# Last groups of the layer-1 backward attention: where wq, K and w2 are loaded and turned

## The chip, the cores and the metric

One core of a Trainium2 chip runs one program. The metric is the device time of a run in microseconds (us), smaller is better. The kernel before took 1139.64 us, median of three runs (1136.17 to 1146.07). One execution was taken by the hardware profiler; all times inside it are us from the start of its span.

Engine names: PE is the matrix engine (PEld its weight loads), DVE the vector engine, ACT the scalar engine, POOL the general-purpose one, SP the engine that issues the loads; SPq is a load issue on SP.

## What is computed

Two layers are run forward and back. The backward pass of attention needs, for each group (batch b, key head kv), the caches V and K and a quarter of wq:

```python
def _A_ref(x, k_cache, v_cache, wq, wo):
    q = (x @ wq).reshape(B, Sq, Hq, Dh).transpose(0, 2, 1, 3)   # B=2, Sq=1, Hq=32, Dh=128
    k = jnp.repeat(k_cache, rep, axis=1)                        # 4 key heads, Sk=16384
    v = jnp.repeat(v_cache, rep, axis=1)
    p = softmax(einsum("bhqd,bhkd->bhqk", q, k) * Dh ** -0.5)
    o = einsum("bhqk,bhkd->bhqd", p, v)
    return o.transpose(0, 2, 1, 3).reshape(B, Sq, Hq * Dh) @ wo
def _B_ref(x, w1, b1, w2, b2):
    return gelu(layernorm(x) @ w1 + b1) @ w2 + b2
...
for layer in (0, 1):
    x = x + _A_ref(layernorm(x), ...)
    x = x + _B_ref(layernorm(x), ...)
```

The outputs are x after both layers and the gradients of a given grad_out by x, the caches and the weights. All data is bfloat16.

## The kernel before, in words

The order of work: forward of both layers, then backward of the MLP of layer 1, of its attention (`attn_bwd`, called once, with l = 1), of the MLP of layer 0 (`w2b`, then `weights_down`), and last a long stage that makes all the gradients of the caches and weights while it runs the attention of layer 0 back.

**Tiles and buffers.** Every load brings one tile of 128 x 4096 bfloat16 (1 MB) into the pool `ld`, which has `NLD` = 7 buffers. All loads are issued by SP, one after the other in the order in which the program allocates the tiles. A new tile takes the free buffer that was released first, and SP waits until the last reader of that buffer's former tile is done. So the place of a load in the program fixes its place in SP's order and the buffer it gets; the time at which it starts is set by the release of that buffer.

**`attn_bwd`** goes over seven groups in the order 0, 4, 3, 1, 5, 2, 6 (group 7 has its tiles kept on the chip and is woven into groups 3 and 1). A group has four chunks of V and four of K. In this document V6.1 is chunk 1 of V of group 6, K6.3 is chunk 3 of its K, and so on. wq comes in quarters, one for each pair of groups with the same kv, and each quarter in two halves: wq1.0 and wq1.4 are the first and second half of quarter 1, wqL.0 and wqL.4 those of the last quarter (kv = 2), w2.0 to w2.6 the tiles of w2 that the next stage needs.

The work is written out by slots, numbered 0 to 127, and then some more until all queues are empty. Slot s transposes a quarter of a V chunk on PE (`emit_T`, L480, eight transposes) and copies it out on ACT or DVE (L159, L162); it runs what the schedule `Sched` has for the slot (`run_slot`); and it makes the scores of slot s - 2 (L726). `later(n, f)` puts f into slot s + n; the queue `q` gives one item every other slot, and one every slot while more than four are waiting or after the last slot. Groups 2 and 6 lie in slots 96 to 127.

- `post` (after a chunk's last scores) makes dX, and `queue_acc` queues two *quads* for the chunk (L512: eight matmuls of dX with K each), and after the last chunk the evacuation of the sum, `reduce` (L527) and `finish`. K of a chunk is loaded when its first quad is run (L469). For the last group, 6, it is loaded already in `post` (`accs[g].pre`), and after the last chunk the first five tiles of w2 are loaded there too (`ahead.load`).
- `finish` puts dq of the group aside. When both groups of a kv are done, `wq_now` deals with its quarter of wq: both halves are loaded in the slot after it (L961), the eight rows of the quarter are turned on DVE (L269, 32 x 32 blocks) in slots +7 to +14, and the two products on PE (L296) are in slots +12 and +17.
- The last quarter is treated apart (`wq_steps`, L986): its halves are loaded from slot 113 on, and its eight rows are turned by transposes on PE (L358, tile `wtq`) and copied out by ACT or DVE. `wq_q` holds these steps; one of them is run in every second slot, so they spread over slots 113 to 125. After group 6 its `finish` copies dq (L1004) and makes the last products (L995, `dn_ps`).
- `ahead` is the object `w2b`. A *unit* of a w2 tile is a forward product on PE (L337) and a turn on DVE (L269) or PE. After the last slots `ahead.some(0, 1)` runs the four units of w2.0, one in each of four slots.

When `attn_bwd` has ended, w2.5 and w2.6 are loaded, the remaining units of w2.0 are run, `banks` clears two accumulators on DVE (L394, L397), and `attn_in_bwd` starts the layer norm backward (L232 on) from dn; the products of w2 follow.

Of the kernel before, what the change touches and what calls it, by code (L numbers as in the profile page):

```python
# [23 lines left out]
def kernel(  # L24
# [36 lines left out]
    DJ = D // 128  # L61
# [5 lines left out]
    NCH = T // TC  # L67
# [3 lines left out]
    CP = TC // 2  # L71
# [3 lines left out]
    NLD = 7  # L75
# [18 lines left out]
    def pt(shape, dtype, name):  # L94
        return ps_tp.tile(shape, dtype, name=name, tag="tp")

    def px(shape, dtype, name):
        return ps_x.tile(shape, dtype, name=name, tag="x")
# [4 lines left out]
    def pm_(shape, dtype, name):  # L103
        return ps_sm.tile(shape, dtype, name=name, tag="sm")
# [35 lines left out]
    def charge(eng, us):  # L140
        load[eng] += us
# [322 lines left out]
    def kv_load(w, g, c):  # L464
        keep = w + str(c) if g == G - 1 else w if (g, c) == (XG, 0) else None
        t = held_tiles[keep] if keep else ld.tile([128, LDW], BF16, name="kv_" + w, tag="ld")
        if keep not in held:
            src = Kv if w == "K" else Vv
            nc.sync.dma_start(t[:].rearrange("p (t d) -> p t d", d=128), src[g, :, c * TC:(c + 1) * TC, :])  # L469
            if keep:  # L470
                held.add(keep)
        return t[:].rearrange("p (t d) -> p t d", d=128)
# [78 lines left out]
    def queue_acc(sc_, a, c_list, tail, coef=None):  # L551
        for c in c_list:
            for q in range(NB // 2):
                sc_.q.append(lambda c=c, q=q: a.quad(c, q, coef))
        if tail:
            def fin():
                a.evac()
                sc_.later(2, a.reduce)
            sc_.q.append(fin)
# [93 lines left out]
    def attn_bwd(l, do_bf, dqT, dn, groups, ahead):  # L653
        sch = Sched()
        wq_q, wq_n = deque(), {}
        slots = []
        for i, g in enumerate(groups):
            for c in range(NCH):
                for b in range(NB):
                    slots.append((g, c, b))  # L660
                    if 2 <= i < 2 + NCH // 2 and c % 2 == 0:
                        slots.append((G - 1, (i - 2) * 2 + c // 2, b))
        kTs, sc, accs = {}, {}, {}
        made = {"n": 0}
        done_g = []
        both = pm_([128, 512], F32, "acc2")
        Acc.third = both[:, 0:256]
        V.memset(both[:, 256:512], 0.0)

        def wq_job(kv):  # L670
            return wq_turned(l, kv, dqT, both[:, 256:512], lambda: px([128, 512], F32, "spg"))

        def wq_now(kv):
            n = wq_job(kv)
            n[1]()
            for f in n[0]:
                sch.later(1, f)
            for j in range(DJ):
                sch.later(7 + j, n[2][j])
            for k in range(2):  # L680
                sch.later(12 + 5 * k, n[3][k])
            if kv == groups[-3] % HKV:
                sch.later(19, wq_sum)

        def wq_sum():
            fin = px([128, DJ, 2], F32, "dn_fin")
            columns(both[:, 256:512], fin)
            V.tensor_copy(out=dn[:], in_=fin[:])

        def post(g, c):  # L690
            dp = sc.pop((g, c))
            PE.matmul(dp[:].rearrange("p h t -> p (h t)"), lhsT=hot3[:],
                      rhs=dlr[:, g, l, :].unsqueeze(2).to_broadcast([128, 8, TC]), start=False, stop=True)
            k = made["n"]
            made["n"] += 1
            ds = dXr[k // 2 % 3][:, :, k % 2]
            ev = e_all[:, g, c * CP:(c + 1) * CP, l, :, :].rearrange("p a h b -> p h a b")
            V.tensor_tensor(out=ds.rearrange("p a h b -> p h a b"),
                            in0=dp[:].rearrange("p h (a b) -> p h a b", b=2), in1=ev, op=ALU.mult)
            charge("D", 0.5)  # L700
            if c == 0:
                def finish(ps, g=g):
                    V.tensor_scalar(out=dqT[:, g, :], in0=ps, scalar1=QSCALE, scalar2=None, op0=ALU.mult)
                    done_g.append(g % HKV)
                    if g == groups[-1]:
                        wq_n["last"][1]()
                        wq_n["last"][3]()
                    elif done_g.count(g % HKV) == 2:
                        wq_now(g % HKV)
                accs[g] = Acc(g, "K", None, finish, 2 if g == G - 1 else groups.index(g) % 2)  # L710
            acc = accs[g]
            if g == groups[-1]:
                accs[g].pre[c] = kv_load("K", g, c)
                if c == NCH - 1:
                    for k in range(NLD - 2):
                        ahead.load(k)
            coef = lambda u: ds[:, u - c * CP].rearrange("p h t -> p (h t)")
            sch.later(2, lambda: queue_acc(sch, acc, [c], c == NCH - 1, coef))

        def score(s):  # L720
            g, c, b = slots[s]
            if b == 0:
                sc[g, c] = px([128, 8, TC], F32, "dp")
            kT = kTs.pop(s)
            for j in range(8):
                PE.matmul(sc[g, c][:, :, b * 8 + j], lhsT=kT[:, j, :], rhs=do_bf[:, g, :], start=(b + j == 0),  # L726
                          stop=False)
            if b == NB - 1:
                post(g, c)

        cv = None
        s = 0
        v_turns = deque(lambda c=c, b=b: turn(held_tiles["V%d" % c][:, b * 1024:(b + 1) * 1024],
                                              lambda: pt([128, 8, 128], BF16, "turn"))
                        for c in range(NCH) for b in range(NB))
        while s < len(slots) + 2 or sch.busy():
            sch.s = s
            if s < len(slots):
                g, c, b = slots[s]
                if g == G - 1:  # L740
                    kTs[s] = kept_vT(c)[:, b * 8:(b + 1) * 8, :]
                else:
                    if b == 0:
                        cv = kv_load("V", g, c)
                    kTs[s] = emit_T(cv, b, True)
                    if s % 3 == 2 and s >= 8 and v_turns:
                        v_turns.popleft()()
                if g == groups[-1] and b == 1 and c == 0:
                    n = wq_n["last"] = wq_steps(l, g % HKV, dqT, dn, lambda: pt([128, 8, 128], BF16, "wtq"),
                                                lambda: px([128, 512], F32, "dn_ps"))  # L750
                    for k, f in enumerate(n[0]):
                        wq_q.append(lambda f=f, k=k, n=n: (f(), n[2][4 * k]()))
                        wq_q.extend(n[2][4 * k + 1:4 * k + 4])
            sch.run_slot(1 if s < len(slots) else 2)
            if 2 <= s < len(slots) + 2:
                score(s - 2)
            if wq_q and (s % 2 == 1 or len(wq_q) > 6):
                wq_q.popleft()()
            if s > len(slots) + 2:
                ahead.some(0, 1)  # L760
            s += 1
        assert not wq_q

# [188 lines left out]
    def wq_turned(l, kv, dqT, acc, bank):  # L952

        hs = slice(kv * 8, kv * 8 + 8)
        box = {}
        Gq = g_tile(8, True)

        def load(j):
            wt = ld.tile([128, LDW], BF16, name="wqt", tag="ld")
            box[j] = wt[:].rearrange("p (j n) -> p j n", j=4)  # L960
            nc.sync.dma_start(box[j], wq_v[:, j:j + 4, kv * D:(kv + 1) * D])  # L961

        def turn_row(j):
            turn32(box[j - j % 4][:, j % 4, :])

        def dq_in():
            for b in range(2):
                V.tensor_copy(out=dq_all[:, hs, 2 * l + b], in_=dqT[:, b * HKV + kv, :])
            spread_g(dq_all[:, hs, 2 * l:2 * l + 2], 0, 8, Gq, bank())

        def part(j):
            products(box[j], Gq, 0, acc[:, 32 * j:32 * j + 128])

        return ([lambda j=j: load(j) for j in (0, 4)], dq_in, [lambda j=j: turn_row(j) for j in range(DJ)],
                [lambda j=j: part(j) for j in (0, 4)])
# [406 lines left out]
    sch = Sched()  # L1382
    kTs, dps, accs, ready = {}, {}, {}, []
# [127 lines left out]
    while 2 * m < NS + 2:  # L1511
# [7 lines left out]
        for k in range(2):  # L1519
            s = 2 * m + k  # L1520
            if s < NS:
                i, b = NCH + s // NB, s % NB
# [38 lines left out]
    i, g = NC - 1, order[-1]  # L1561
# [58 lines left out]
```

## Time and profile before

| what | value |
|---|---|
| runs | 1139.64, 1136.17, 1146.07 us |
| span of the profiled execution, first to last instruction | 1138.1 us |
| mean granted PE clock | 0.857 |
| PE, DVE, ACT busy | 915.9 (80%), 619.8 (54%), 534.0 (47%) us |
| moved by DMA | 449.20 MB, mean 395 GB/s |
| the chain that ended last, by engine | PE 45%, DMA 35%, DVE 10%, issue 5%, ACT 4% |
| median time from issue to landing of a K tile, over the program | 13.0 us |

How to read it: the profiled execution has only its span as its own time; the median of the runs is 1.5 us above it. Busy shares are means over stages with different limits, so a stage is read by its own window. `attn_bwd` lies from about 490 to 662 us, `w2b` and `weights_down` up to about 733 us, the last stage from there to the end.

### The profile page before, as it was taken

The page shows a single profiled execution, that of the slowest core. Times are in us where ns is not written, and L with a number is a line of the kernel's source. Part 1 is how long each engine was busy: PE and PEld are TensorE (multiplying, and loading weights), DVE is VectorE, ACT ScalarE, POOL GpSimd, SP SyncE. Part 2 cuts the span into 40 slices and gives each one's busy share as a digit, 9 for nine tenths or more (in the row PEclk, how much of TensorE's full clock was granted, in tenths as well). Part 3 has the DMA queues.
Part 4 walks back from the last instruction along what each step waited for, and adds up shares of the span by engine and source line. Part 5 has one row for each costly group of instructions (what it writes and reads, how often), then busy time and mean ns, then how long its engine had stood idle before and what let it go on. Part 6 is the DMA issues. An engine that isn't in the chain of part 4 may idle for free.

```text
span 1138.1 us, 38123 instructions
## 1 busy us (share of the span) xinstructions
PE 915.9 (80%) x16766; PEld 674.7 (59%) x16767; DVE 619.8 (54%) x1363; ACT 534.0 (47%) x1356; POOL 70.2 (6%) x124
## 2 busy tenths in 40 slices
PE   4979795468888975789887678888898897899996
PEld 3867674358766754778765567755545454455552
DVE  1545451180545523654442246678798767786876
ACT  0544351005544420434333214468697766676764
POOL 0000000000000000000000000022121111111210
PEclk9988895567999875899998678999999978897978
DMA  8999999999999979999999699998999999999997
GB/s 371 423 425 425 424 424 413 395 413 423 423 425 423 412 288 404 388 422 421 399 413 393 232 380 309 370 386 302 403 419 421 421 419 424 423 411 421 423 385 290
DMA packets 104183, 449.20 MB, mean 395 GB/s; under 512 B 7238, under 2 KB 11334, under 8 KB 66896
## 3 DMA queue, kind: packets, MB, share of 16 engines
q1 hardware_dynamic: 86672, 354.46, 77.6%
q0 software_dynamic: 17344, 92.29, 19.6%
q8 instruction: 131, 2.15, 0.7%
q14 instruction: 36, 0.29, 0.1%
HBM read 348.14 MB, written 98.58 MB: 393 GB/s over the span
## 4 chain that ended last, share of the span: by engine, by line
PE 45%; DMA 35%; DVE 10%; issue 5%; ACT 4%; POOL 0%; SPq 0%; DVEq 0%; ACTq 0%; POOLq 0%
DMA kv_V<-in_A_v_cache_dram 13%; PE tp L480 10%; DMA wt<-in_B_w_dram 5%; PE acc_all L512 4%; PE tpm L1527 4%; DMA kv_K<-in_A_k_cache_dram 4%; PE xm L1336 4%; DMA wt<-in_A_wo_dram 3%; DMA out_dram<-keepK 3%; DMA keepK<-in_A_v_cache_dram 3%; PE sc L633 3%; PE xm L1250 2%; PE wtp L358 2%; PE dp L1389 2%; PE dp L726 2%
## 5 line engine op out<-in xcount | busy, mean ns | idle before, releaser
L159 ACT COPY kT<-tp 128x512 int32<-128x512 int32 x200 | 117.4, 587 | 298.4 <-PE tp L480 289.1
L162 DVE COPY kT<-tp 128x1024 bf16<-128x1024 bf16 x168 | 114.9, 690 | 141.8 <-PE tp L480 130.4
L480 PE MATMUL tp<-ident,kv_K 128*128 128x128 bf16 x1728 | 142.0, 230 | 6.9 <-DMA kv_K<-in_A_k_cache_dram 6.8
L480 PEld LDWEIGHTS <-kv_K 128*128 128x128 bf16 x1728 | 107.8, 103 | 7.7 <-DMA kv_K<-in_A_k_cache_dram 7.5
L170 DVE CAST big<-xm 128x512 bf16<-128x512 f32 x133 | 86.3, 684 | 19.3 <-PE xm L1336 14.3
L167 ACT CAST big<-xm 128x512 bf16<-128x512 f32 x151 | 82.1, 595 | 25.0 <-PE xm L1336 14.8
L633 PE MATMUL sc<-qT_bf,kT 128*128 128x8 bf16 x2048 | 91.5, 171 | 0.1
L633 PEld LDWEIGHTS <-kT 128*128 128x128 bf16 x2048 | 75.7, 97 | 26.7 <-issue 20.8
L337 PEld LDWEIGHTS <-wt 128*128 128x128 bf16 x1920 | 57.4, 104 | 54.7 <-issue 17.8
L167 ACT CAST keepV<-xm 128x512 bf16<-128x512 f32 (+1 forms) x137 | 75.0, 594 | 29.5 <-PE xm L1336 18.5
L480 PE MATMUL tp<-ident,kv_V 128*128 128x128 bf16 x864 | 70.2, 227 | 14.1 <-DMA kv_V<-in_A_v_cache_dram 12.2
L597 ACT ACTIVATE e_all<-sc,negm 128x64 bf16<-128x64 f32 x256 | 77.2, 343 | 1.0 <-DVE negm L592 1.0
L170 DVE CAST keepV<-xm 128x512 bf16<-128x512 f32 (+1 forms) x101 | 65.9, 684 | 18.9 <-PE xm L1336 12.7
L269 DVE STREAM_TRANSPOSE wt<-wt 128x512 int32<-128x512 int32 x104 | 63.6, 674 | 14.2 <-PE w2b_f L337 11.0
L512 PE MATMUL acc_all<-kv_V,e_all 128*16 128x256 bf16 x864 | 46.0, 293 | 28.7 <-DMA kv_V<-in_A_v_cache_dram 14.4
L159 ACT COPY wt<-wtp 128x512 int32<-128x512 int32 x72 | 40.3, 587 | 57.0 <-PE wtp L358 54.1
L480 PEld LDWEIGHTS <-kv_V 128*128 128x128 bf16 x864 | 55.2, 101 | 16.2 <-DMA kv_V<-in_A_v_cache_dram 13.1
L597 ACT ACTIVATION_READ_ACCUMULATOR e_all<-sc,negm 128x1 f32 x256 | 59.8, 234 | 0.0
L167 ACT CAST keepK<-xm 128x512 bf16<-128x512 f32 x98 | 53.0, 596 | 14.1 <-PE xm L1336 7.5
L1389 PE MATMUL dp<-wdo,kT 128*128 128x64 bf16 x896 | 52.8, 206 | 0.0
L358 PE MATMUL wtp<-ident,wt 128*128 128x128 bf16 x576 | 47.8, 244 | 4.9 <-ACT wt L159 2.6
L1336 PE MATMUL xm<-QmK,blk 64*128 64x512 bf16 x256 | 48.8, 444 | 2.3 <-ACT keepV L167 1.0
(387 smaller groups left out, 1564.4 us busy)
## 6 DMA issues: line engine op xcount, KB each, us to landing
kv_K<-in_A_k_cache_dram SPq DMA_DIRECT2D x81, 1024.0 KB, 13.0
kv_V<-in_A_v_cache_dram SPq DMA_DIRECT2D x81, 1024.0 KB, 12.9
wt<-in_B_w_dram SPq DMA_DIRECT2D x42, 1024.0 KB, 12.9
wt<-in_A_wo_dram SPq DMA_DIRECT2D x32, 1024.0 KB, 9.6
out_dram<-big POOLq DMA_DIRECT2D x26, 1024.0 KB, 18.9
out_dram<-keepV POOLq DMA_DIRECT2D x19, 1024.0 KB, 20.7
out_dram<-keepK POOLq DMA_DIRECT2D x17, 1024.0 KB, 17.8
wt<-in_A_wq_dram SPq DMA_DIRECT2D x16, 1024.0 KB, 11.0
```

Of the source, the lines that this page charges most:

```text
L159: S.copy(out=dst.bitcast(I32), in_=src.bitcast(I32))
L162: V.tensor_copy(out=dst, in_=src)
L167: S.copy(out=dst, in_=src)
L170: V.tensor_copy(out=dst, in_=src)
L269: V.transpose(out=w, in_=w)
L358: PE.transpose(tp[:, o, :], view[:, o * 128:(o + 1) * 128], ident[:])
L480: PE.transpose(tp[:, j, :], cv[:, b * 8 + j, :], ident[:])
L512: PE.matmul(self.acc[cg:cg + 16, :], lhsT=coef(u), rhs=self.cv[:, t:t + 2, :].rearrange("p t d -> p (t d)"), start=False, stop=True, tile_ ...
L597: S.activation(out=e_all[:, g, f * half:(f + 1) * half, l, h, :], in_=sc[g][f][:, h, :].rearrange("p (a b) -> p a b", b=2), func=ACT.Exp, ...
L633: PE.matmul(sc[g][f][:, :, t % TH], lhsT=kT[:, j, :], rhs=q_bf[:, g, :], start=True, stop=True)
L1336: PE.matmul(pss[k][:], lhsT=blk[p:p + 64, o + 2 * h + k // 2, :], rhs=Qm[p:p + 64, :, :].rearrange("p a b -> p (a b)"), start=True, stop=T ...
L1389: PE.matmul(dp[:, :, t:t + 4], lhsT=kT[:, j, :], rhs=wd[:, :, x:x + 4], start=(b + j == 0), stop=False)
```

## The change

All of it is in `attn_bwd`.

- The quarters 0, 3 and 1 of wq are loaded and turned half by half: half k is loaded in slot +1 + 4k, its four rows are turned in slots +4 + 4k to +7 + 4k, its product is in slot +9 + 4k. The sum of the products (`wq_sum`) comes in slot +15 in place of +19.
- K of group 6 is no longer loaded in `post`; like K of the other groups it is loaded when its first quad is run. Its quads are queued one slot earlier.
- The last quarter's steps begin in slot 120 in place of 113, and one is run in every slot.
- The five w2 tiles are loaded after the quads of K6.3, from the same queue. The four units of w2.0 are no longer run in the last slots; one of them is run in `finish`, between the copy of dq and the last products, the other three after `attn_bwd`.

```diff
         def wq_now(kv):
             n = wq_job(kv)
             n[1]()
-            for f in n[0]:
-                sch.later(1, f)
-            for j in range(DJ):
-                sch.later(7 + j, n[2][j])
             for k in range(2):
-                sch.later(12 + 5 * k, n[3][k])
+                sch.later(1 + 4 * k, n[0][k])
+                for j in range(4):
+                    sch.later(4 + 4 * k + j, n[2][4 * k + j])
+                sch.later(9 + 4 * k, n[3][k])
             if kv == groups[-3] % HKV:
-                sch.later(19, wq_sum)
+                sch.later(15, wq_sum)
...
                     if g == groups[-1]:
                         wq_n["last"][1]()
+                        ahead.some(0, 1)
                         wq_n["last"][3]()
...
             acc = accs[g]
-            if g == groups[-1]:
-                accs[g].pre[c] = kv_load("K", g, c)
+            coef = lambda u: ds[:, u - c * CP].rearrange("p h t -> p (h t)")
+            def queue():
+                queue_acc(sch, acc, [c], False, coef)
+                if g == groups[-1] and c == NCH - 1:
+                    sch.q.append(lambda: [ahead.load(k) for k in range(NLD - 2)])
                 if c == NCH - 1:
-                    for k in range(NLD - 2):
-                        ahead.load(k)
-            coef = lambda u: ds[:, u - c * CP].rearrange("p h t -> p (h t)")
-            sch.later(2, lambda: queue_acc(sch, acc, [c], c == NCH - 1, coef))
+                    queue_acc(sch, acc, [], True)
+
+            sch.later(1 if g == groups[-1] else 2, queue)
...
-                if g == groups[-1] and b == 1 and c == 0:
+                if g == groups[-1] and b == 0 and c == 2:
                     n = wq_n["last"] = wq_steps(l, g % HKV, dqT, dn, lambda: pt([128, 8, 128], BF16, "wtq"),
                                                 lambda: px([128, 512], F32, "dn_ps"))
...
-            if wq_q and (s % 2 == 1 or len(wq_q) > 6):
+            if wq_q:
                 wq_q.popleft()()
-            if s > len(slots) + 2:
-                ahead.some(0, 1)
             s += 1
```

The order in which SP issues its loads, from V6.0's neighbourhood on (up to K2.0 the two orders differ in one place: wq3.4 stands ahead of V5.2 before, and behind it after):

```
before: ... K2.0 wq1.0 wq1.4 V6.0 K2.1 wqL.0 K2.2 V6.1 K6.0 K2.3 wqL.4 V6.2 K6.1 V6.3 K6.2 K6.3 w2.0 w2.1 ...
after:  ... K2.0 wq1.0 V6.0 K2.1 wq1.4 K2.2 V6.1 K2.3 V6.2 wqL.0 V6.3 K6.0 wqL.4 K6.1 K6.2 K6.3 w2.0 w2.1 ...
```

## The prediction

> **What bounds the kernel now.** I read the granted clock and the DMA rows of the page first, then the windows of the stages around the change (columns: us, busy time of PE, PEld, DVE, ACT, POOL with counts, granted PE clock, DMA share, GB/s):
>
> ```profile
> 490.00:612.00 122.00, 105.66 (x2436) 87.28 (x2432) 53.44 (x124) 46.05 (x81) 0.00 (x0) 1.00 1.01 414
> 612.00:622.00 10.00, 7.46 (x89) 5.90 (x89) 1.60 (x3) 1.76 (x3) 0.00 (x0) 0.51 0.97 384
> 622.00:660.00 38.00, 24.04 (x427) 19.22 (x424) 10.24 (x21) 9.06 (x16) 0.00 (x0) 0.72 0.72 260
> 660.00:690.00 30.00, 25.31 (x654) 22.21 (x655) 14.30 (x36) 7.41 (x13) 0.00 (x0) 0.73 1.02 369
> 690.00:733.00 43.00, 34.55 (x867) 30.88 (x867) 29.75 (x94) 18.52 (x35) 0.71 (x1) 0.92 0.91 331
> ```
>
> Up to 612 the attention is bound by its loads: DMA share 1.01, and a tile of 1.05 MB at 414 to 425 GB/s takes 2.5 us. From 622 to 660 the rate is 260 GB/s, and PE is not the bound either (24.04 of 38 us, at clock 0.72). Both wait for each other. The timeline of SP's issues says why (start, duration, issue, count; a duration over 0.4 spans waits between merged issues):
>
> ```profile
> 603.28 0.38 SPq L986 DMA_DIRECT2D wqt<-in_A_wq_dram  x1
> 607.43 0.33 SPq L469 DMA_DIRECT2D kv_K<-in_A_k_cache_dram  x1
> 608.17 0.33 SPq L469 DMA_DIRECT2D kv_V<-in_A_v_cache_dram  x1
> 620.26 2.23 SPq L469 DMA_DIRECT2D kv_K<-in_A_k_cache_dram  x2
> 624.03 0.38 SPq L986 DMA_DIRECT2D wqt<-in_A_wq_dram  x1
> 631.60 0.33 SPq L469 DMA_DIRECT2D kv_V<-in_A_v_cache_dram  x1
> 638.29 0.33 SPq L469 DMA_DIRECT2D kv_K<-in_A_k_cache_dram  x1
> 638.72 0.37 SPq L469 DMA_DIRECT2D kv_V<-in_A_v_cache_dram  x1
> 642.81 8.90 SPq L469 DMA_DIRECT2D kv_K<-in_A_k_cache_dram  x2
> ```
>
> In SP's order these are wqL.0, K2.2, V6.1, then K6.0 and K2.3, wqL.4, V6.2, K6.1, V6.3, K6.2 and K6.3. After V6.1 SP issues nothing for 12.1 us. The chain of waits goes through these loads:
>
> ```profile
> 603.28 14.46 DMA wqt<-in_A_wq_dram
> 622.16 7.58 DMA kv_K<-in_A_k_cache_dram
> 631.60 4.61 DMA kv_V<-in_A_v_cache_dram
> 638.72 8.10 DMA kv_V<-in_A_v_cache_dram
> 653.54 6.65 DMA wt<-in_B_w_dram
> 664.06 1.90 PE dn_ps L995 x64
> ```
>
> wqL.0, K2.3, V6.2, V6.3, w2.0, then the products that end the attention. V6.2, with an empty queue, takes 4.61 us from issue to landing; in a stream one lands every 2.5. The order of the program gives the reason: V6.2's buffer is released by V6.1's last transposes in slot 119 and it is needed in slot 120, a lead of one slot; wqL.4 has three (116 to 119); V6.3 stands behind K6.1, which waits for the product of wq1.0 in slot 120. Both halves of wq1 and wqL.0, and K6.0, hold buffers long before their use.
>
> **Part by part.**
>
> *Order and leads (removes the stall).* With the new order I take for each load the slot that releases its buffer and the slot that needs it: V6.1 110 to 116, K2.3 111 to 118, V6.2 114 to 120, wqL.0 115 to 120, V6.3 116 to 124, K6.0 117 to 124, wqL.4 119 to 124, K6.1 120 to 128, K6.2 121 to 130, K6.3 123 to 132, w2.0 126 to 137. The smallest lead is five slots, where it was one. In time: the 50th load of this stage lands at 612.88 (V6.0 before: PE's transposes start at 612.88 after waiting 4.56 us for it); after the change the 50th is K2.1. At 2.5 us each, V6.1 lands at 620.4, V6.2 625.4, wqL.0 627.9, K6.0 632.9, wqL.4 635.4, K6.3 642.9, w2.0 645.4. Every release comes earlier than the landing before it: V6.2's and wqL.0's at about 615 (slots 114 and 115, just after K2.1), K6.0's at about 622, K6.1's at 626, w2.0's in slot 126, about 638 to 640 against the 640.8 that a continuous stream needs (645.4 less 4.6). So the queue never runs dry, and nothing of the old 15 us of idle DMA (38 us x (1 - 260/425)) should be left.
>
> *The end of the attention.* K6.3's two quads start at 642.9 and 643.4 (0.54 each at half clock: 615.32 to 615.86). Before, from the second quad (661.42) to the last products (664.06) it took 2.64 us. One unit of w2.0 (0.4 on PE, its row at 660.24) comes between; its turn on DVE (0.65) lies beside the products. Products from 646.5 to 648.4, against 665.96: **-17.5 us**. The w2.0 wait of 3.41 us at 660.24 that stood between the last quads is in this.
>
> *Moved units of w2.0.* Three turns of 0.65 us (row "DVE wt L269 x2", 1.30) now stand on DVE after the sum of dn and before `banks` and the layer norm, which are on the chain. **+2.0 us**.
>
> *The last quarter in slots 120 to 127.* Same 64 transposes, now one row per slot beside the V transposes. From wqL.0 on PE has, at half clock, 15 groups of eight transposes (0.81 each: 616.09 to 616.90), eight quads (0.54), nine score groups (0.25), a product (0.95) and some 1.5: 21.3 us; at full clock (0.54, 0.33, 0.21) about 13. From 627.9 that ends at 641 to 649. K6.3 bounds it at 644 if the clock comes back as it did before (half from 615 to about 622, then full: 5 us of 21.3 cold, the rest at 0.62, ends at 643). I take 0 and keep **+5 us** for the range.
>
> *wq half by half.* The same 24 turns and six products; each half's three slots of lead cost nothing as long as SP's order puts it ahead of a tile that is needed in an earlier slot: wq3.0 (needed in 90) stands before V5.2 (88), wq3.4 (94) before V5.3 (92), wq1.0 (112) before V6.0 (112, first in the slot), wq1.4 (116) before K2.2 (115). If one came late, the turn would hold back the copies of kT behind it on DVE, and with them PE: at most one tile time, 2.5 us, for each of six halves; 0 taken.
>
> *Loads of w2 and after.* At 2.5 us each, w2.4 to w2.6 land 7 to 12 us after the products end, where it was 4 to 9; w2.4 is needed 12.4 us after that end (first PE row of it at 678.33), the others later, so 0. w2.0 lands 14.8 us earlier and the products end 15.5 earlier with the turns counted, so the stages to 733 move as a whole whether loads (share 1.02) or engines bound them; the last stage moves with them.
>
> *Clock against rule.* PE's clock is 1.00 at 605 to 610 and 0.66 in the next 5 us, where PE idles 4.56 us in one piece. The Trainium skill, "TensorE: Matmul & The Clock Gate", section "HAM oscillation", asks for no PE-idle gap over about 3.4 us. By that rule the new waits, 2.5 us apart, would keep the clock up, and the end would come about 1.5 us sooner; the sum stays with the half-clock rows.
>
> *A rule against the change.* "DMA: Bandwidth & Descriptors", section "Rules for kernel authors", says to issue a DMA early and wait late. K6.0 to K6.3 and w2.0 are issued later in the program; by this rule each could show its setup, 4.61 - 2.5 = 2.1 us in the trace, and the sum would be 10 us worse. Here the release of a buffer, not the place of the issue, starts a load, so I do not follow it.
>
> Sum: -17.5 + 2.0 = **-15.5 us**. On the profiled span of 1138.1 that is 1122.6; the median of the runs stands 1.5 above that span, so 1124.
>
> **The rivals.**
>
> 1. *PE becomes the bound of the tail*: cold all the way from wqL.0, -15.5 + 5 = -10.5, 1129. For it: clock 0.51 and 0.72 in the old tail. Against: there it had idle gaps of 3 to 4.6 us; it recovered within 7 us of dense work.
> 2. *The stall only moves*: the halves' short leads in wq0, wq3 and wq1 cost up to 6 x 2.5 = 15 us and the sum is about zero, 1139. For it: DVE copies in order. Against: the order of SP above.
> 3. *Slower*: wqL.0's steps begin in the slot of its load. If its release in slot 115 came after 623.3 (8 us later than I find; 627.9 less 4.6), V6.3's transposes and all releases behind would follow it in single file: 4.6 of load and 1.2 of PE work in place of 2.5, 3.3 us for each of the eight loads wqL.0, V6.3, K6.0, wqL.4, K6.1 to K6.3, w2.0: +26, in sum +11, 1150. It decides from five such loads on. Against: V6.0 lands before 612.88 and its four transposes need no later tile than K2.1.
>
> **How the numbers follow.** Forecast 0.70, rival 1 0.14, rival 2 0.08, rival 3 0.08. A run tells about 1% from no change, so faster means under 1128.2. Of the forecast (own range 1117 to 1131: 3 us more if the clock stays up, runs 3 to 4 us apart, turns or clock against me) 0.65 lies under that, of rival 1 0.05: faster 0.70; same 0.20 (0.05 of the forecast, 0.09 of rival 1, 0.06 of rival 2); slower 0.10. The range 1117 to 1134 leaves out rivals 2 and 3 and little else.
>
> **What would show it.** Right: DMA near 420 GB/s without a hole up to the landing of w2.0 near 645; SP issuing with several loads outstanding; dn_ps near 646; three turns of w2.0 between the sum of dn and `banks`. Wrong: SP idle for more than 5 us between 612 and 640 (rival 3), PE waits for `wqt` or DVE waits before 612 (rival 2), or dn_ps after 651 at a clock of 0.5 without DMA waits (rival 1).

## The result, and the profile after

| | before | after |
|---|---|---|
| median of the runs in one job (4 each) | 1138.89 us (1136.17 to 1146.07) | 1126.39 us (1125.16 to 1128.56) |
| span of the profiled execution | 1138.1 us | 1123.4 us |
| sum of dn on DVE (L997) | 665.99 | 648.24 |
| first clear of `banks` (L394) | 666.26 | 650.46 |
| first product of w2 backward (`w2b_d`) | 671.55 | 655.62 |
| first load of the last stage | 720.25 | 703.69 |
| from there to the end | 417.8 | 419.7 |

The ratio is 0.9877 (95% interval 0.985 to 0.9903): 1.2% faster, 12.5 us by the medians, 14.7 us by the two profiled spans. In a second job the changed kernel took 1124.67 us against 1138.73, ratio 0.9868 (0.9844 to 0.9892). The prediction was 1124 us.

The windows of the changed kernel (same columns as before: us, busy time of PE, PEld, DVE, ACT, POOL with counts, granted PE clock, DMA share, GB/s):

```profile
490.00:612.00 122.00, 106.72 (x2452) 88.19 (x2448) 54.74 (x126) 45.86 (x81) 0.00 (x0) 1.00 1.01 413
612.00:622.00 10.00, 6.34 (x98) 4.56 (x97) 2.82 (x5) 2.38 (x5) 0.00 (x0) 0.67 1.02 425
622.00:646.00 24.00, 19.90 (x436) 16.04 (x428) 8.25 (x20) 8.57 (x15) 0.00 (x0) 0.93 1.02 403
646.00:660.00 14.00, 10.98 (x299) 10.13 (x299) 8.04 (x22) 2.93 (x5) 0.00 (x0) 0.66 1.03 394
660.00:676.00 16.00, 13.24 (x384) 11.98 (x384) 8.39 (x23) 5.54 (x10) 0.00 (x0) 0.89 1.03 369
```

The stage of 38 us at 260 GB/s is gone: from 612 to the end of the attention the DMA share is 1.02 to 1.03, where it is 1.01 in the 122 us before. SP's timeline shows the loads coming without the hole (start, duration, issue, count; a duration over 0.4 spans waits between merged issues):

```profile
607.50 0.33 SPq L469 DMA_DIRECT2D kv_V<-in_A_v_cache_dram  x1
608.24 0.33 SPq L469 DMA_DIRECT2D kv_K<-in_A_k_cache_dram  x1
617.08 0.33 SPq L469 DMA_DIRECT2D kv_V<-in_A_v_cache_dram  x1
618.14 0.38 SPq L986 DMA_DIRECT2D wqt<-in_A_wq_dram  x1
622.45 0.33 SPq L469 DMA_DIRECT2D kv_V<-in_A_v_cache_dram  x1
624.58 0.33 SPq L469 DMA_DIRECT2D kv_K<-in_A_k_cache_dram  x1
626.99 0.38 SPq L986 DMA_DIRECT2D wqt<-in_A_wq_dram  x1
627.97 4.70 SPq L469 DMA_DIRECT2D kv_K<-in_A_k_cache_dram  x3
638.48 19.90 SPq L331 DMA_DIRECT2D wt<-in_B_w_dram  x9
```

These are V6.1, K2.3, V6.2, wqL.0, V6.3, K6.0, wqL.4, K6.1 to K6.3, then w2. SP issues nothing for 8.5 us after K2.3 and for 5.8 us after K6.3, and still the DMA share stays at 1.02, because several loads are outstanding at both places. In the kernel before, the long pause after V6.1 (608.5 to 620.3) was no hole either: the DMA share was 1.02 up to 620. The queue ran dry later, where SP could issue only one or two loads at a time (windows of the kernel before):

```profile
612.00:620.00 8.00, 5.46 (x65) 4.08 (x65) 1.02 (x2) 1.41 (x3) 0.00 (x0) 0.50 1.02 419
628.00:632.00 4.00, 1.99 (x32) 1.47 (x32) 0.66 (x2) 0.34 (x1) 0.00 (x0) 0.59 0.69 268
636.00:638.00 2.00, 1.75 (x40) 1.55 (x44) 0.00 (x0) 0.59 (x1) 0.00 (x0) 0.50 0.00 0
648.00:652.00 4.00, 4.00 (x73) 3.08 (x73) 0.95 (x3) 0.59 (x1) 0.00 (x0) 0.50 0.02 10
```

So the length of SP's pause alone tells nothing. The chain of waits in the changed kernel:

```profile
599.44 13.96 DMA kv_K<-in_A_k_cache_dram
618.14 10.08 DMA wqt<-in_A_wq_dram
638.48 7.58 DMA wt<-in_B_w_dram
646.11 0.39 PE w2b_f L337 x8
646.50 1.71 PE dn_ps L995 x64
648.46 1.90 DVE wt L269 x3
650.46 0.48 DVE w2b_d L394
```

It goes through three loads that are 7.6 to 14 us under way, the time in a full queue; before it went through V6.2 with 4.61, a queue that was nearly empty. w2.0 is the last load that the attention waits for, PE waits 1.28 us for its landing, and the three turns of w2.0 (1.90 us) now stand between the sum of dn and the clears.

### The profile page after: what moved, and what is told of

The parts are those of the page before. It is cut to its first block, busy times and chain, and to the rows that moved or that the text cites. A ratio compares the mean times of both kernels' runs of the same rounds, so it can differ in the third digit from the quotient of the medians.

```text
span 1123.4 us, 38122 instructions
## 1 busy us (share of the span) xinstructions
PE 907.1 (81%) x16766; PEld 668.2 (59%) x16767; DVE 619.5 (55%) x1364; ACT 532.4 (47%) x1355; POOL 70.1 (6%) x124
## 4 chain that ended last, share of the span: by engine, by line
PE 46%; DMA 34%; DVE 11%; issue 4%; ACT 4%; POOL 0%; DVEq 0%; SPq 0%; ACTq 0%; POOLq 0%
DMA kv_V<-in_A_v_cache_dram 13%; PE tp L480 9%; DMA wt<-in_B_w_dram 5%; DMA kv_K<-in_A_k_cache_dram 5%; PE tpm L1527 4%; PE xm L1336 4%; PE acc_all L512 4%; DMA wt<-in_A_wo_dram 3%; PE xm L1250 3%; PE sc L633 3%; PE dp L1389 2%; PE wtp L358 2%; DMA out_dram<-keepxV 2%; DMA keepK<-in_A_v_cache_dram 2%; PE dp L728 2%
## 5 line engine op out<-in xcount | busy, mean ns | idle before, releaser
L633 PEld LDWEIGHTS <-kT 128*128 128x128 bf16 x2048 | 76.1, 98 | 27.7 <-issue 21.5
L337 PEld LDWEIGHTS <-wt 128*128 128x128 bf16 x1920 | 57.0, 104 | 51.7 <-issue 14.7
L480 PE MATMUL tp<-ident,kv_V 128*128 128x128 bf16 x864 | 67.9, 223 | 7.3 <-DMA kv_V<-in_A_v_cache_dram 5.8
L170 DVE CAST keepK<-xm 128x512 bf16<-128x512 f32 x69 | 44.8, 684 | 9.2 <-PE xm L1336 5.4
## 6 DMA issues: line engine op xcount, KB each, us to landing
out_dram<-keepK POOLq DMA_DIRECT2D x17, 1024.0 KB, 17.5
```

The source lines that it names most:

```text
L170: V.tensor_copy(out=dst, in_=src)
L337: PE.matmul(fps[:, o0 + o, :].rearrange("p (a b) -> p a b", b=2), lhsT=wv[:, j, o * 128:(o + 1) * 128], rhs=x[:, j0 + j, :].unsqueeze(1).t ...
L480: PE.transpose(tp[:, j, :], cv[:, b * 8 + j, :], ident[:])
L633: PE.matmul(sc[g][f][:, :, t % TH], lhsT=kT[:, j, :], rhs=q_bf[:, g, :], start=True, stop=True)
```

## The experiments

The theory: a load of this stage starts when a slot releases its buffer and is needed by a later slot; where this lead is short, SP's releases and PE go in lock-step, and the three edits together raise the least lead (the slots between the two) from one slot to five. The main rival: each edit takes its own share of the gain, about a third, whatever the leads are.

In what follows the leads are worked out from the order of the program, as in the prediction. A single sum of dn turned out to be a poor measure, since the stage itself began at times up to 5.4 us apart (first `dl_ps` product 490.43 to 495.86). So I also count the bytes of the trace's DMA records from that product on, take the moment at which 36 tiles of 1.05 MB have been moved (583 to 592 us) and measure from there to the sum of dn ("end part"). Up to w2.0 every kernel but "four more" has the same loads in it. This measure was chosen after the runs had been seen; the last two runs test it. Each kernel has one profile, apart from the two that were run again; a ratio is to the kernel before in the same job (medians 1138.73 to 1141.88 us).

| kernel | loads with a lead under 5 (slots) | sum of dn | end part | time, us | ratio to before (95%) |
|---|---|---|---|---|---|
| changed | none | 648.24 | 64.4 | 1126.39 | 0.9877 (0.985 to 0.9903) |
| changed, again | none | 649.50 | 65.7 | 1124.67 | 0.9868 (0.9844 to 0.9892) |
| halves undone | 4 | 655.07 | 64.5 | 1127.83 | 0.9858 (0.9804 to 0.9912) |
| halves undone, again | 4 | 656.86 | 65.2 | 1130.33 | 0.9913 (0.9883 to 0.9943) |
| K early | 4, 4, 4 | 652.30 | 67.2 | 1127.94 | 0.987 (0.9825 to 0.9916) |
| last quarter early | 4, 4, 4 | 653.72 | 68.4 | 1130.35 | 0.9889 (0.9838 to 0.994) |
| one buffer fewer | 4, 4, 4 | 656.21 | 68.5 | 1129.95 | 0.9904 (0.9867 to 0.9942) |
| K and w2 alone | 4, 4, 4, 4 | 657.20 | 70.3 | 1130.32 | 0.9916 (0.9886 to 0.9945) |
| last quarter alone | 4, 4, 4, 4 | 658.09 | 74.5 | 1130.56 | 0.9917 (0.9887 to 0.9947) |
| halves alone | 3, 3, 3, 4 | 660.12 | 75.8 | 1135.67 | 0.9967 (0.9942 to 0.9992) |
| two buffers fewer | 4, 4, 2, 3, 4, 3, 4, 3, 4 | 661.10 | 77.2 | 1137.83 | 0.9982 (0.9951 to 1.0013) |
| before | 3, 3, 1, 4 | 665.99 | 82.6 | 1138.89 | 1 |

The end part is not the same work in all rows. In the kernels with the later w2 tiles three turns of w2.0 stand behind the sum of dn; in the last quarter alone, the halves alone and the kernel before they stand ahead of it. So from the sum of dn to the first clear of `banks` it takes 2.2 us in the former and 0.3 in the latter. Up to the clears the changed kernel takes 66.6 us, K and w2 alone 72.5, the last quarter alone 74.8, the halves alone 76.1, two buffers fewer 79.4 and the kernel before 82.9: the order is the same, but the whole gain is 16.3 us in place of 18.2.

### One part taken back at a time

The half-by-half loading undone (the products follow in slots +12 and +17 and the sum in +19, as before):

```diff
             for k in range(2):
-                sch.later(1 + 4 * k, n[0][k])
-                for j in range(4):
-                    sch.later(4 + 4 * k + j, n[2][4 * k + j])
-                sch.later(9 + 4 * k, n[3][k])
+                sch.later(12 + 5 * k, n[3][k])
```

with both loads in slot +1 and the eight turns in +7 to +14.

> The quarters 0, 3 and 1 of wq are loaded and turned as before, the rest is changed. The sum of dn, which ends the attention, was at 665.99 us before and is at 648.24 after the change. Leads theory (a load costs nothing while the release of its buffer leads its use by enough slots): the least lead in the last two groups is four slots (wqL.4) in place of five, so nearly all of the gain stays: sum of dn at 648 to 651, time 1126 to 1129. Rival of shares (each of the three parts brings about a third of the 17.75 us): sum of dn near 654, time near 1131.

K of the last group loaded early again:

```diff
             acc = accs[g]
+            if g == groups[-1]:
+                accs[g].pre[c] = kv_load("K", g, c)
```

> K of the last group is loaded as early as before, the rest is changed. Leads theory: least lead four slots (K2.3, wqL.0, wqL.4), and K6.0 and K6.1 stand in the stream ahead of tiles that are needed earlier, 2.5 us each: sum of dn at 648 to 652, time 1126 to 1130. Rival of shares: sum of dn near 654, time near 1131.

The last quarter from slot 113, every second slot:

```diff
-                if g == groups[-1] and b == 0 and c == 2:
+                if g == groups[-1] and b == 1 and c == 0:
...
-            if wq_q:
+            if wq_q and (s % 2 == 1 or len(wq_q) > 6):
```

> The steps of the last quarter of wq begin in slot 113 and are taken every second slot as before, the rest is changed. Leads theory: least lead four slots (K2.3, wqL.4, V6.2): sum of dn at 648 to 652, time 1126 to 1130. Rival of shares: sum of dn near 654, time near 1131. Clock theory (the gain comes from a PE that stays at full clock because the transposes of the last quarter stand close together): half clock from 612 on as before, sum of dn at 655 or later.

Measured sums of dn: 655.07, 652.30 and 653.72, so +6.8, +4.1 and +5.5 over the changed kernel. Taken alone that looks like the rival's equal shares. The end parts say otherwise: 64.5, 67.2 and 68.4 against 64.4 to 65.7, so 0, some 2 and some 3 us. Together that is far under 18; no part holds a third of the gain. The sums of dn that the leads theory had named (up to 651 or 652) were missed all the same. The clock theory of the third run needed half clock from 612 on and a sum at 655 or later; the granted clock was 0.60 from 612 to 622, but 0.88 from 622 to 646 (0.67 and 0.93 in the changed kernel). What the first of the three loses, it loses before the 36th tile (see the last experiment).

### One part alone

The half-by-half loading alone, in the kernel before:

```diff
             for k in range(2):
-                sch.later(12 + 5 * k, n[3][k])
+                sch.later(1 + 4 * k, n[0][k])
+                for j in range(4):
+                    sch.later(4 + 4 * k + j, n[2][4 * k + j])
+                sch.later(9 + 4 * k, n[3][k])
```

> The kernel before, with the quarters 0, 3 and 1 of wq loaded and turned half by half, and nothing else changed. Leads theory: the least lead rises from one slot to three (K2.3, wqL.4, V6.2), so some holes stay: sum of dn at 652 to 660 (before 665.99, after 648.24), time 1128 to 1135. Rival of shares: a third of the 17.75 us, sum of dn near 660, time near 1133.

The later last quarter alone, in the kernel before:

```diff
-                if g == groups[-1] and b == 1 and c == 0:
+                if g == groups[-1] and b == 0 and c == 2:
...
-            if wq_q and (s % 2 == 1 or len(wq_q) > 6):
+            if wq_q:
```

> The kernel before, with the steps of the last quarter of wq begun in slot 120 and one in every slot, and nothing else changed. Leads theory: least lead four slots in place of one, though K6.0 and K6.1 stand ahead of tiles needed earlier and w2.0 is waited for among the last quads: sum of dn at 649 to 654, then no three turns behind it; time 1125 to 1131. Rival of shares: sum of dn near 660, time near 1133.

The later K and w2 alone: the changed kernel with both the other parts taken back, by the first and third diffs of the section before.

> The change of K of the last group and of the w2 tiles alone; all quarters of wq as before. Leads theory: least lead four slots in place of one: sum of dn at 648 to 654, time 1126 to 1132. Rival of shares: sum of dn near 660, time near 1133.

Measured: the sums of dn are 660.12, 658.09 and 657.20, all later than the leads theory had named, and the first at the rival's 660. The end part shrinks by 6.7, 8.1 and 12.2 us, in sum 27 where all three together bring 18.2; up to the clears by 6.8, 8.1 and 10.4, in sum 25 where all three bring 16.3. The times say the same with less room: 0.3, 0.8 and 0.8% alone, in sum 2.0%, against 1.2 to 1.3% together. So the parts overlap, which equal shares do not: each removes much of the same stall, and what is left after two of them is little. The order by leads holds, but a lead of four costs more than I had expected: the last two stand some 5 to 8 us behind the changed one at the clears. The windows of the halves alone, around the old hole:

```profile
622.00:646.00 24.00, 16.58 (x344) 13.56 (x342) 8.12 (x16) 6.77 (x13) 0.00 (x0) 0.85 0.91 331
```

331 GB/s where the changed kernel has 403. And four leads of four slots are not always the same: the last quarter alone has a wait that K and w2 alone lacks, second line here (waits of PE from 600 to 662 in the last quarter alone: who waited, for whom, us in total, times, longest):

```profile
PE tp L480 <- DMA kv_V<-in_A_v_cache_dram: 7.7, 4, 4.2
PE acc_all L512 <- DVE wqt L269: 2.8, 1, 2.8
```

A turn of wq on DVE stood in the way of a quad for 2.8 us. But of the 4.2 us by which the two end parts differ, 1.9 are only the turns of w2.0 behind the sum of dn, and K and w2 alone waits 5.4 us for K where the last quarter alone waits 1.4. Where the remaining 2.3 us come from is not shown. So the list of leads orders the kernels; it does not give the microseconds.

### The same order with fewer buffers

The changed kernel, with one or two of the load buffers taken by an unused tile from slot 96 (and 100) to 136. Work and order stay as they are, only leads become shorter:

```diff
+            if s == 96:
+                taken = ld.tile([128, LDW], BF16, name="taken", tag="ld")
+                nc.gpsimd.memset(taken[:, 0:2], 0.0)
+            if s == 136:
+                V.memset(taken[:, 0:2], 0.0)
             s += 1
```

> The changed kernel, with one of the seven buffers taken away from slot 96 on, until the attention ends. Leads theory: least lead four slots (K2.3, wqL.0, wqL.4) in place of five, five in place of six for V6.1: sum of dn at 648 to 652, time 1126 to 1130; that is, one buffer is spare, two are not.

> The changed kernel, with two of the seven buffers taken away from slots 96 and 100 on, until the attention ends; no other work is added but four tiny clears. Leads theory: the least lead falls to two slots (V6.1) and three (K2.3, wqL.0, wqL.4), so DMA has holes again between 612 and 645 and about half of the gain is lost: sum of dn at 653 to 662, time 1131 to 1139. Shares and clock theories: order and work are those of the change, so the gain stays: sum of dn at 648 to 650, time 1126 to 1128.

Measured: end part 68.5 with one buffer fewer, 77.2 with two. That one buffer would be spare was wrong: it costs 3 to 4 us. With two fewer 12.8 of the 18.2 us are lost again and the time is that of the kernel before, within its interval. Windows of the kernel with two fewer:

```profile
622.00:646.00 24.00, 16.64 (x320) 13.95 (x321) 6.33 (x14) 6.36 (x11) 0.00 (x0) 0.78 0.83 321
646.00:656.00 10.00, 6.12 (x107) 4.62 (x106) 1.12 (x2) 2.34 (x4) 0.00 (x0) 0.84 0.66 229
```

The slow rate is back (321, then 229 GB/s) with the new order of instructions in place. This is the strongest run of the study: it takes nothing but buffers, so the new order brings its gain only with buffers that come free early enough. The clock does not explain the loss: it is lower than in the changed kernel from 622 to 646 (0.78 against 0.93), but PE is busy for only 16.64 of the 24 us, and its longest waits from 612 to 660 are for loads (K 7.4, V 3.6, wq 3.0 us in total). The opposite run, the kernel before with more buffers, was not made; that its stall is the same one rests on the like rates (260 GB/s) and on the leads.

### Four more loads

Are the loads now the bound of the whole stage? Four loads of 1.05 MB that nothing reads, in slots 97, 101, 105 and 109:

```diff
+            if s in (97, 101, 105, 109):
+                more = ld.tile([128, LDW], BF16, name="more", tag="ld")
+                nc.sync.dma_start(more[:].rearrange("p (t d) -> p t d", d=128), Kv[0, :, 0:TC, :])
             s += 1
```

> The changed kernel with four more loads of 1 MB in slots 97, 101, 105 and 109, which nothing reads. If loads bound the changed attention to its end, all four show: 4 x 2.5 = 10 us, sum of dn at 657 to 660, time near 1136. If PE or the chain of releases had become the bound (rival 1 of the prediction), at most 4 us show, time 1126 to 1130.

The window and, from DVE's timeline, the sum of dn (start, duration, line and operation, then the idle time before it and its cause):

```profile
612.00:656.00 44.00, 30.64 (x619) 24.09 (x606) 13.83 (x30) 12.13 (x21) 0.00 (x0) 0.84 1.02 410
```

```profile
658.13 0.17 DVE L1000 TENSOR_TENSOR dn<-dn,dn_ps 128x16 f32<-128x16 f32 x1 [0.99 <-PE dn_ps L998]
```

658.13 - 648.24 = 9.9 us for four tiles, 2.5 us each, the full rate (410 GB/s at share 1.02); 1135.8 us, ratio 0.9947 (0.9919 to 0.9975). In the changed kernel the attention is bound by its loads to its last one, and PE has room at a clock of 0.84.

### The turns in the gaps of the layer norm

An attempt to win back the 2 us of the three turns: one more unit in `finish`, one in the gap of the layer norm, the last one and `banks` after the copy of its result.

```diff
-                        ahead.some(0, 1)
+                        ahead.some(0, 2)
...
-    w2b.some(0)
-    w2b.banks()
-    g2 = attn_in_bwd(1, g3, dn1, lambda: w2b.some(1, 1), lambda: w2b.some(1, 2))
+    g2 = attn_in_bwd(1, g3, dn1, lambda: w2b.some(1, 1), lambda: (w2b.some(1, 2), w2b.some(0, 1)))
     V.tensor_copy(out=gM_all[:, 0:DJ, lsl(0)], in_=g2[:])
+    w2b.banks()
+    w2b.some(0)
```

> The changed kernel, with two units of w2.0 in place of one between the copy of dq and the last products, one in the gap in which the vector engine waits for the layer norm's sum, one after it, and the two accumulators cleared behind the layer norm. The 2.0 us that the three turns cost in the sum of the prediction, and the 0.9 us of the clears, lie on the chain in the changed kernel: if so, the first product of w2 (at 655.62 after the change) comes 1.5 to 2.5 us sooner, and the time is 1124 to 1126. If they lay beside other work: no difference.

Measured: 1126.72 us (ratio 0.9871, 0.9837 to 0.9905), no gain. From the sum of dn to the first product of w2 it took 8.0 us (649.51 to 657.52), against 7.4 (648.24 to 655.62) and 6.7 in the two profiles of the changed kernel. DVE's timeline shows why:

```profile
649.51 0.17 DVE L997 TENSOR_TENSOR dn<-dn,dn_ps 128x16 f32<-128x16 f32 x1 [0.61 <-PE dn_ps L995]
653.56 0.71 DVE L269 STREAM_TRANSPOSE wt<-wt 128x512 int32<-128x512 int32 x1 [3.46 <-PE w2b_f L337]
654.19 0.12 DVE L240 TENSOR_SCALAR lb_nm<-lb_ps 128x4 f32<-128x4 f32 x1
```

The turn was put ahead of the layer norm's step (L240) in DVE's order, and waited 3.46 us for its unit's forward product, which stood on PE behind other units. The expectation failed on a wait of my own making. Whether a better placing wins the 2 us was not tried.

### The halves and the kernel itself once more

The remaining question was where the kernel with the halves undone loses its 6.8 us.

> The changed kernel with wq loaded and turned as before (whole quarters, products in slots +12 and +17), a second time. In its first profile the sum of dn came 6.8 us later than in the changed kernel, but the attention stage itself began 3.7 us later there (first dl_ps product 495.56 against 491.86), and from the moment at which 36 tiles of 1.05 MB had been moved after that product to the sum of dn it took 64.50 us, against 64.37 in the changed kernel. Theory (one load with a lead of four slots costs nothing; the late start was scatter between executions): from 36 tiles to the sum of dn 64 to 66.5 us, and a time within 0.4% of the changed kernel run beside it. Rival (the 6.8 us were the price of the whole quarters): over 69 us, sum of dn at 653 or later with the stage beginning near 492, and a time 4 to 7 us above the changed kernel.

> The changed kernel itself, beside the one with the whole quarters, to see how far two executions of one program differ. Theory: from 36 tiles moved to the sum of dn 64 to 66 us (64.37 and, in the kernel that is the same up to there, 64.81 in two profiles), whatever the start of the stage is; start of the stage between 490.5 and 495.5; time 1124 to 1129 us. Rival: the part from 36 tiles on scatters by 4 us or more as well, and then the 2.7 to 6 us between the kernels with three and four short leads say nothing.

Measured: the end part is 65.2 us with the halves undone and 65.7 in the changed kernel. On this the theory holds: given the two other parts, one lead of four costs nothing that can be seen, and three profiles of the order of the changed kernel (with the one of the turns in the gaps, 64.8) agree within 1.3 us. So the 67.2 of K early, a single profile, is barely apart from no cost; 68.4 and above are apart.

The rest of the expectation failed. The late start was not scatter between two executions, for it came again (495.86; the changed kernel 491.38), and the time is 1130.33 us against 1124.67, 0.5% more and not within 0.4%. Of the 7.4 us between the two sums of dn, 4.5 are there when the stage begins and 3.4 more are added up to the 36th tile, of which 2.5 in its first 12; the end part gives 0.5 back. But the edit first changes what an engine executes at the first load of wq, later than these 12 tiles (they are through at 521.7 in the changed kernel, and SP issues the first wq load at 522.2). The windows of earlier work, in which the two programs do not differ, in the changed kernel (its first profile) and then with the halves undone, again:

```profile
385.00:395.00 10.00, 8.28 (x177) 6.57 (x174) 4.32 (x12) 3.28 (x8) 0.00 (x0) 1.00 1.01 422
395.00:405.00 10.00, 9.64 (x212) 7.68 (x211) 6.58 (x13) 5.60 (x32) 0.00 (x0) 1.00 1.03 398
```

```profile
385.00:395.00 10.00, 7.54 (x128) 5.89 (x124) 3.01 (x9) 2.35 (x4) 0.00 (x0) 0.71 1.01 419
395.00:405.00 10.00, 9.87 (x179) 8.37 (x181) 5.02 (x10) 6.49 (x35) 0.00 (x0) 0.78 0.82 319
```

PE was granted 0.71 and 0.78 of its clock there, has 179 records of products in the second window where the other has 212, and the loads fell to 319 GB/s. Three profiles start late (halves undone twice, K and w2 alone 494.84), all three of kernels with whole quarters and the later K and w2; the other profiles begin between 490.43 and 492.73. But the low clock does not tell them apart: in the first profile of the halves undone it lies at 375 to 385 (0.66), with 1.00 in the two windows shown, and the kernel before has 0.71 at 365 to 375 and begins at 491.68. So why these three start late stays open, and so does whether the half-by-half loading is worth its 0.5% by itself: the end part says no, and so does the ratio of the first job (0.9858); the six runs of each in the second job say yes.

## Why the prediction was right

**The stall** (-17.5): the sum of dn moved by 17.75 us. wqL.0 and w2.0 landed at 628.22 and 646.06 where 627.9 and 645.4 had been worked out, and the last products ran from 646.3 to 648.2, predicted 646.5 to 648.4. The step "at 2.5 us each from the 50th load on" was right because the queue did not run dry; the four more loads confirm the 2.5 us, the fewer buffers confirm that leads are what keeps it full.

That it comes out to 0.2 us is luck. The prediction went from K6.3's quads, 0.54 us each at half clock, through 2.64 us and a unit of w2.0 to 646.5. In the trace both quads together took 0.61 us, dq was ready at 645.25 (L1004), and PE waited for w2.0:

```profile
643.08 0.61 PE L512 MATMUL acc_all<-kv_K,dX 128*16 128x256 bf16 x16 [0.60 <-DMA kv_K<-in_A_k_cache_dram]
644.95 0.30 DVE L1004 CAST dq_all<-dqT 128x8 bf16<-128x8 f32 x2
646.11 0.39 PE L337 MATMUL w2b_f<-h_all,wt 128*128 128x32 bf16 x8 [1.28 <-DMA wt<-in_B_w_dram]
```

So the end was set by the landing of w2.0, 0.7 us later than worked out, and not by the path from K6.3, which was shorter than taken; the two cancel. The second profile of the changed kernel has its sum of dn at 649.50, 1.3 us later. One reading of the prediction was off as well: the 12.1 us in which SP issues nothing are not the stall, since the DMA share was 1.02 up to 620; the empty stretches come after 628. The sum does not use the 12.1 us.

**The turns** (+2.0): 1.90 us on the chain. The clears came 15.8 us earlier, predicted 15.5.

**The rest moves as a whole**: 15.9 us at the first product of w2, 16.6 at the first load of the last stage, 14.7 at the end. The last stage took 1.9 us longer in this profile; over all profiles of this study it took 415.6 to 421.2, so no cause is sought.

**Costs set at 0**: the last quarter in slots 120 to 127 cost nothing, though rival 1's premise came true in part. The clock was 0.67 from 612 to 622 and 0.66 after 646, but 0.93 between, and the loads, not PE, ended last. The halves' turns held nothing up (rival 2): 413 GB/s up to 612, against 414. Rival 3 needed wqL.0's release after 623.3; wqL.0 was issued at 618.14.

**The clock against the rule.** The Trainium skill, "TensorE: Matmul & The Clock Gate", section "HAM oscillation", had let one expect the clock to stay up, since the new waits are shorter than about 3.4 us. Windows of 5 us of the changed kernel:

```profile
605.00:610.00 5.00, 3.21 (x81) 2.52 (x72) 2.54 (x5) 1.17 (x2) 0.00 (x0) 1.00 1.03 418
610.00:615.00 5.00, 2.59 (x32) 1.99 (x33) 0.21 (x1) 0.59 (x1) 0.00 (x0) 0.60 1.04 423
615.00:620.00 5.00, 3.79 (x60) 2.70 (x57) 2.82 (x5) 1.76 (x3) 0.00 (x0) 0.71 1.02 422
620.00:625.00 5.00, 3.98 (x77) 2.94 (x78) 0.00 (x0) 1.17 (x2) 0.00 (x0) 0.66 1.01 413
625.00:630.00 5.00, 4.56 (x118) 3.61 (x116) 2.43 (x5) 2.34 (x4) 0.00 (x0) 1.00 1.02 409
```

The longest PE waits there are 2.60 us (before V6.0's transposes), 1.99 and 1.43, and the clock fell to 0.60 all the same. The measurement decides: the clock did not stay up. Half-clock rows were right for the last products (1.87 us, 1.89 before), and not for K6.3's quads, which ran at full clock.

**Early issue against late release.** The Trainium skill's rule to issue a DMA early and to wait for it late ("DMA: Bandwidth & Descriptors", section "Rules for kernel authors") had been set aside with the reason that here a buffer's release starts a load. The run with K early tests it: issuing K6.0 to K6.3 earlier brought no gain in the end part (67.2 against 64.4 to 65.7).

**What I had wrong** lies beside the sum: three or four leads of four slots are not harmless (some 2 to 8 us, measured to the clears), so the reserve that I saw in the new order is about one slot, not one buffer.

## What to carry to other kernels

Where loads share a ring of buffers and one queue in order, list for every load the step that frees its buffer and the step that needs it; the shortest distances mark the stall, and buffers that are filled long before their use are what makes them short. Load later what is needed later, and spread a block's loads like its use. Compare edits over a stretch that carries the same bytes and begins where the programs begin to differ, for the start of a stage can differ by 4 to 5 us where the programs have not yet differed. See too that the stretch ends behind work that an edit only moves.

## What the runs showed of the hardware

- The granted clock of PE fell to 0.60 with no idle gap of PE over 2.60 us (610 to 615 in the changed kernel), and was 1.00 again at 625.
- In work that no edit touches, the granted clock fell at different times: from 385 to 395 us it was 1.00 in the changed kernel and 1.00 and 0.71 in the first and second profile of the halves undone, the first of which has 0.66 from 375 to 385.
- SP issued nothing for 8.5 us (changed) and 11.8 us (before) while the loads under way kept the DMA share at 1.02.
